# A softmax convolution, a two-dimensional Fourier mix and an MLP on one core: the low halves of the normalised rows stored as one run with shifted weight tables, the first column's fold on ScalarE, one more addition a batch on VectorE, and the mask of the weight scale taken in PSUM

## The chip, the core and the metric

The kernel runs on one core of one Trainium2 chip. The metric is the device time of one execution in microseconds (us). The engines are TensorE (PE; its weight loads are shown as PEld), VectorE (DVE), ScalarE (ACT) and GpSimd (POOL); SyncE (SP) issues every DMA. Each engine works through its own list of instructions in order and waits on semaphores for the others.

## The reference

The input is x of 8 batches, 4224 positions and 192 columns. All of it is float32 in and out.

```python
# 1. a causal convolution of 7 taps, weights by softmax, one set for each of 8 heads of 24 columns
w = softmax(weight_gen, axis=-1)                      # (8, 4224, 8, 7)
x = einsum('bshk,bskhg->bshg', w, windows_of(x, 7))   # (8, 4224, 192)
# 2. the real part of a Fourier transform over positions and columns, added
u = x + real(fft(fft(x, axis=1), axis=2))
# 3. rows normalised, then an MLP 192 -> 768 -> 192, added
un = (u - mean(u)) / sqrt(var(u) + 1e-6)
out = u + maximum(un @ w_ch1, 0) @ w_ch2
```

## The kernel before

**Tiling.** The 4224 positions of a batch are 33 rows r on 128 partitions. They are worked in nine groups g (or chunks c): eight of four rows, 128x768 elements, and a last one of a single row, 128x192. `conv(b)` (L710) makes the seven products of a chunk, `pr`, mostly on VectorE (128x768), and GpSimd adds them into `u`; with `DVE_ADDS` (L50) the first of the six additions of a chunk runs on VectorE instead, in two halves of 128x384 through PSUM tiles `ps` (`add_in_psum`, L701). Before the change that is so in chunks 2 to 7 of batch 1 alone. Then the chunk's two pairs of mirrored rows are folded into `sm`: column 0 stands apart, since columns 1 to 191 are read backwards. TensorE multiplies `sm` by a Fourier table (`pg`), the result goes through DRAM (`g_d`) and comes back as `g`; `transform(b)` (L913) and `mix(b, g)` (L961) finish the transform (`pp`, `eo`) and add it to `u`.

**Norm and MLP.** `norm(b, g)` (L987) normalises a group into `un` and splits it into two float16 parts, `hl`: the high part of the 192 columns, then the rest. Before the change the rest stands crosswise: block 1 of `hl` is high columns 128 to 191 beside low columns 128 to 191, block 2 is low columns 0 to 127. So the subtraction takes two GpSimd instructions. One transposing DMA turns `hl` into `ht`, three blocks of 128 rows for the first matrix product `ph` (tables `w1h0`, `w1l0`, `w1h1`, `w1l1` by `pieces`, L1054). ScalarE and VectorE make the hidden part `hh`, and TensorE multiplies it by the second matrix into `po`. Groups are numbered n = 9b + g. Up to n = 6 the second product is float32 with the table `w2f`; from then on it is float16 with `w2h` and `w2l`.

**Weight scales.** The matrices get a power of two as scale (`weight_scale`, L547): VectorE takes the largest word of each partition (`mx`), masks its exponent bits, takes the largest over the three pieces, TensorE carries it across partitions (`mr`), and VectorE makes the scale `sc` out of it. For the first matrix this runs at 65 to 75 us, for the second (`split_w2`, L632) at 167 to 191 us, in the middle of batch 0's MLP and batch 1's convolution.

**Order.** The code only records instructions. `plan` (L219) then places them on the engines by costs for each (`cost`, L192), dependencies, buffers and the seven PSUM banks that all products share, and `emit` (L385) writes them in that order. So a change of one instruction gives the engines another order everywhere after it. As all instructions are issued by `emit`, the profile puts them on one line, L408, and groups are told apart by tiles.

Of the kernel before, what the change touches and what calls it, by code (L numbers as in the profile page):

```python
# [11 lines left out]
F16 = mybir.dt.float16  # L12
# [37 lines left out]
DVE_ADDS = {(1, c): 1 for c in range(2, NC)}  # L50
HOLD3 = 3
WIRE = 0.5

F32_GROUPS = 7
# [405 lines left out]
def tile_dynconv_fnet_mlp(  # L460
# [52 lines left out]
    w2f = cpool.tile([P, NH, D], F32, name="w2f")  # L513
# [33 lines left out]
    def weight_scale(words, bits, nm):  # L547

        mask, unit, least, up, down = {32: (0x7F800000, 1.0, 4.0 * 2 ** 23, 257.0, -3.0),
                                       64: (0x7FF00000, 8.0, 900.0 * 2 ** 20, 1153.0, -899.0)}[bits]  # L550
        n = len(words)
        mx = cpool.tile([P, 2 * n + 2], F32, name=f"mx_{nm}")
        for i, word in enumerate(words):
            nc.vector.tensor_reduce(out=mx[:, i:i + 1], in_=word.bitcast(F32), axis=AX.X, op=ALU.max, apply_absolute_value=True)
        ex = mx[:, n:2 * n].bitcast(I32)
        nc.vector.tensor_scalar(out=ex, in0=mx[:, 0:n].bitcast(I32), scalar1=mask, scalar2=None, op0=ALU.bitwise_and)
        m1, m2 = mx[:, 2 * n:2 * n + 1], mx[:, 2 * n + 1:2 * n + 2]
        nc.vector.tensor_reduce(out=m1, in_=ex, axis=AX.X, op=ALU.max)
# [151 lines left out]
    def conv(b):  # L710
# [53 lines left out]
        for grp in groups:  # L764
# [222 lines left out]
    def norm(b, g):  # L987
# [46 lines left out]
        for t in range(T):  # L1034
# [5 lines left out]
        nc.gpsimd.tensor_tensor(out=hl[:, 0:T, 2 * P:3 * P], in0=un[:, 0:T, 0:P],  # L1040
                                in1=hl[:, 0:T, 0:P], op=ALU.subtract)
        last_lo[NG * b + g] = nc.gpsimd.tensor_tensor(out=hl[:, 0:T, D:2 * P], in0=un[:, 0:T, P:D],
                                                      in1=hl[:, 0:T, P:D], op=ALU.subtract)
# [43 lines left out]
    def first_products(n, hidden):  # L1087
# [229 lines left out]
```

## Time and profile before

| What | Before |
|---|---|
| Median of 3 runs | 1097.79 us (1095.75 to 1098.76) |
| Profiled execution | 1100.12 us, its span 1098.3 us |
| TensorE, VectorE busy | 1065.1 us, 961.5 us |
| ScalarE, GpSimd busy | 786.7 us, 871.5 us |
| TensorE's granted clock, mean | 0.991 |

The busy time of an engine is the time in which it had an instruction under way. TensorE's matmuls overlap, so a mean duration there is longer than the spacing of two matmuls. In names such as `hl<-un,hl` the tile that is written stands first.

### The profile page before, as it was taken

To read this page: it belongs to the slowest core of one execution; us is meant where nothing else is said; L and a number is where in the kernel's file an instruction comes from. 1 tells how busy PE (TensorE), PEld (TensorE's weight loads), DVE (VectorE), ACT (ScalarE), POOL (GpSimd) and SP (SyncE) were. 2 spreads that over 40 slices of the span, in tenths; PEclk is the share of its full clock that TensorE was granted. 3 is DMA by queue.
4 is the path that set the end of the run, shared out by engine and by line. 5 is a ranking of instruction groups with operands and counts; after the bars stand their busy time and mean duration, and the time that the engine had idled before them with its cause. 6 is when DMAs were issued, how large, how long until landed. Compare 5 with 4: busy or idle time off the path is not lost.

```text
span 1098.3 us, 23862 instructions
## 1 busy us (share of the span) xinstructions
PE 1065.1 (97%) x8596; PEld 807.9 (74%) x8596; DVE 961.5 (88%) x1737; ACT 786.7 (72%) x2385; POOL 871.5 (79%) x759
## 2 busy tenths in 40 slices
PE   7899997999999999999999999999999999999998
PEld 5477785788575867677777867687777777787767
DVE  7999899789999999999999999999999998345443
ACT  4666774569855797868785888778786888579841
POOL 4989799399999999699979999799969999202210
PEclk8999998999999999999999999999999999999999
DMA  8453142624475246715465266616553423622421
GB/s 300 150 161 93 50 106 89 178 63 102 113 215 135 67 130 194 155 58 138 108 204 110 71 140 182 166 53 148 111 162 95 92 65 79 135 57 70 90 57 48
DMA packets 166125, 130.20 MB, mean 119 GB/s; under 512 B 119533, under 2 KB 142710, under 8 KB 166006
## 3 DMA queue, kind: packets, MB, share of 16 engines
q1 hardware_dynamic: 166006, 128.67, 45.2%
q8 instruction: 68, 1.11, 0.4%
q14 instruction: 51, 0.42, 0.1%
HBM read 60.38 MB, written 39.43 MB: 91 GB/s over the span
## 4 chain that ended last, share of the span: by engine, by line
PE 43%; DVE 20%; POOL 19%; issue 12%; DMA 4%; ACT 2%; SPq 1%; POOLq 0%; DVEq 0%
PE po L408 18%; PE ph L408 17%; POOL u L408 15%; DVE pr L408 6%; DVE u L408 3%; DVE hh L408 3%; POOL hl L408 3%; PE eo L408 2%; PE pp L408 2%; DVE wp L408 2%; POOL sm L408 1%; PE pg L408 1%; DMA x_sb<-in_x_dram 1%; DVE mx_w L408 1%; DMA g<-g_d 1%
## 5 line engine op out<-in xcount | busy, mean ns | idle before, releaser
L408 POOL TENSOR_TENSOR u<-u,pr 128x768 f32<-128x768 f32 (+1 forms) x396 | 655.2, 1679 | 29.2 <-DVE pr L408 17.8
L408 PE MATMUL po<-w2h,hh 128*128 128x192 f16 x2832 | 416.6, 246 | 5.2 <-DVE hh L408 4.2
L408 PEld LDWEIGHTS <-hh 128*128 128x128 f16 x4248 | 364.1, 98 | 48.4 <-DVE hh L408 5.6
L408 PE MATMUL ph<-ht,w1h 128*128 128x512 f16 (+1 forms) x1296 | 391.2, 363 | 1.6 <-DMA ht<-hl 1.0
L408 DVE TENSOR_TENSOR pr<-x_sb,wp 128x768 f32<-128x768 f32 (+1 forms) x409 | 347.9, 875 | 17.6 <-POOL u L408 15.1
L408 PE MATMUL po<-w2l,hh 128*128 128x192 f16 x1416 | 347.7, 246 | 0.0
L408 ACT ACTIVATE hh<-ph 128x512 f16<-128x512 f32 (+2 forms) x400 | 221.2, 589 | 127.4 <-PE ph L408 83.8
L408 DVE SCALAR_TENSOR_TENSOR hh<-ph,hh 128x512 f16<-128x512 f32 (+1 forms) x358 | 233.0, 677 | 63.5 <-ACT hh L408 63.0
L408 PE MATMUL ph<-ht,w1l 128*128 128x512 f16 (+2 forms) x696 | 230.6, 359 | 0.0
L408 PEld LDWEIGHTS <-w1h 128*128 128x128 f16 x1296 | 127.5, 99 | 108.0 <-issue 27.4
L408 POOL TENSOR_TENSOR hl<-un,hl 128x512 f16<-128x512 f32 (+1 forms) x138 | 116.5, 859 | 70.4 <-issue 38.0
L408 ACT ACTIVATE un<-u,rs 128x192 f32<-128x192 f32 x264 | 127.0, 538 | 23.1 <-POOL rs L408 15.0
L408 ACT ACTIVATE junk<-u,st 128x192 f16<-128x192 f32 x252 | 114.2, 454 | 4.4
L408 ACT ACTIVATE junk<-u 128x192 f16<-128x192 f32 x252 | 90.8, 361 | 35.9 <-DVE u L408 32.9
L408 PEld LDWEIGHTS <-w1l 128*128 128x128 f16 (+1 forms) x864 | 64.2, 97 | 51.4 <-issue 18.5
L408 DVE SCALAR_TENSOR_TENSOR u<-po,isc,u 128x384 f32<-128x384 f32 (+1 forms) x122 | 72.8, 597 | 20.5 <-PE po L408 20.1
L408 PE MATMUL eo<-cs_sb,pq 97*128 97x97 f32 x544 | 86.2, 273 | 0.2 <-ACT pq L408 0.2
L408 PEld LDWEIGHTS eo<-cs_sb,pq 97*128 97x128 f32 x544 | 78.2, 191 | 5.8 <-issue 0.4
L408 POOL TENSOR_TENSOR sm<-u 128x382 f32<-128x382 f32 (+1 forms) x128 | 75.2, 608 | 4.2 <-ACT u L408 4.2
L408 PE MATMUL po<-w2f,hh 128*128 128x192 f32 x336 | 76.9, 333 | 0.0
L408 DVE TENSOR_TENSOR u<-u,eo 128x380 f32<-128x380 f32 (+3 forms) x160 | 71.7, 487 | 0.6
L408 PEld LDWEIGHTS po<-w2f,hh 128*128 128x128 f32 x336 | 61.8, 194 | 13.1 <-issue 0.7
(92 smaller groups left out, 1162.5 us busy)
## 6 DMA issues: line engine op xcount, KB each, us to landing
out_dram<-u SPq DMA_DIRECT2D x64, 384.0 KB
x_sb<-in_x_dram SPq DMA_DIRECT2D x48, 384.0 KB
x_sb<-in_x_dram SPq DMA_DIRECT2D x8, 864.0 KB
g<-g_d SPq DMA_DIRECT2D x40, 162.0 KB
g_d<-gt SPq DMA_DIRECT2D x32, 195.0 KB
g_d<-gt SPq DMA_DIRECT2D x32, 189.0 KB
g<-g_d SPq DMA_DIRECT2D x40, 144.0 KB
w<-in_weight_gen_dram SPq DMA_DIRECT2D x6, 924.0 KB
```

Source lines behind the costliest of these rows:

```text
L408: ins = getattr(getattr(nc, op.engine), op.call)(*map(found, op.args), **{n: found(a) for n, a in op.kw.items()}).ins
```

## The change

There are four edits. (1) **Halves one behind the other:** from n = 9 on, one GpSimd subtraction writes the low part of all 192 columns behind the high part. The rows of `ht` are thereby another set, so two copies of the high table with shifted rows are made (`w1s`, four DMAs from `w1h0` and `w1h1`, in the place of `w2f`, which no later group reads). (2) **Column 0's fold** is done by ScalarE in two instructions of 128x1 with the mirrored value as bias, in all eight batches; GpSimd did it in one of 128x2. (3) **One addition a batch:** chunk 3 of batches 2 to 7 has its first addition on VectorE through PSUM. (4) **The scale's mask:** the maximum over the three pieces is taken first, on unmasked words; the mask and what follows it work on two columns of the PSUM bank that holds `mr`.

```diff
+DVE_ADDS = {**{(1, c): 1 for c in range(2, NC)}, **{(b, 3): 1 for b in range(2, 8)}}
+ACT_FOLDS = range(8)
+LINEAR = 9
...
     def weight_scale(words, bits, nm):
-        ex = mx[:, n:2 * n].bitcast(I32)
-        nc.vector.tensor_scalar(out=ex, in0=mx[:, 0:n].bitcast(I32), scalar1=mask, scalar2=None, op0=ALU.bitwise_and)
-        m1, m2 = mx[:, 2 * n:2 * n + 1], mx[:, 2 * n + 1:2 * n + 2]
-        nc.vector.tensor_reduce(out=m1, in_=ex, axis=AX.X, op=ALU.max)
+        m1 = mx[:, n:n + 1]
+        nc.vector.tensor_reduce(out=m1, in_=mx[:, 0:n], axis=AX.X, op=ALU.max)
         row = pst("ph", [P, P], F32, f"mr_{nm}")
         nc.tensor.matmul(row, lhsT=m1.broadcast_to([P, P]), rhs=ident32, start=True, stop=True)
-        nc.vector.tensor_reduce(out=m2, in_=row, axis=AX.X, op=ALU.max)
-        nc.vector.tensor_scalar_max(out=m2, in0=m2, scalar1=least)
+        top, word = row[:, 0:1], row[:, 1:2].bitcast(I32)
+        nc.vector.tensor_reduce(out=top, in_=row, axis=AX.X, op=ALU.max)
+        nc.vector.tensor_scalar(out=word, in0=top.bitcast(I32), scalar1=mask, scalar2=None, op0=ALU.bitwise_and)
+        nc.vector.tensor_scalar_max(out=top, in0=word, scalar1=least)
...
     def conv(b):
-                    last_fold[b] = nc.gpsimd.tensor_tensor(out=sm[:, :, 0], in0=u[:, 0:2, 0], in1=u[:, 3:1:-1, 0],
-                                                           op=ALU.add)
+                    if b in ACT_FOLDS:
+                        for j in range(2):
+                            nc.scalar.activation(sm[:, j, 0:1], u[:, j, 0:1], AF.Identity, bias=u[:, 3 - j, 0:1])
...
     def norm(b, g):
+        if NG * b + g >= LINEAR:
+            last_lo[NG * b + g] = nc.gpsimd.tensor_tensor(out=hl[:, 0:T, D:2 * D], in0=un[:, 0:T], in1=hl[:, 0:T, 0:D], op=ALU.subtract)
+        else:
...
+    def linear_tables():
+        w1s = cpool.tile([P, 2, DFF], F16, name="w1s", tag="w2f")
+        for dst, src in ((w1s[0:64, 0], w1h1[0:64]), (w1s[64:P, 0], w1h0[0:64]),
+                         (w1s[0:64, 1], w1h0[64:P]), (w1s[64:P, 1], w1h1[64:P])):
+            nc.sync.dma_start(dst, src)
+        tables[:] = w1s[:, 1], w1s[:, 0]
+    def pieces():
+        return ((w1h0, 0), (w1l0, 0), (tables[0], 2), (tables[1], 1), (w1l1, 1))
...
     def mlp(n):
+        if n == LINEAR:
+            linear_tables()
```

The order that the plan makes of it is shown at three places. The first is VectorE at the second matrix's scale (`mx_w`, `mr_w`), beside chunk 7 of batch 1's convolution (`pr_7`); before:

```order
L408 TENSOR_REDUCE mx_w_391_1749<-w2f_937 128x1
L408 TENSOR_TENSOR pr_7_4_428_1860<-x_sb_71,wp_166_643 128x768
L408 TENSOR_SCALAR mx_w_391_1749<-mx_w_391_1749 128x3
L408 TENSOR_REDUCE mx_w_391_1749<-mx_w_391_1749 128x1
L408 TENSOR_TENSOR gt_4_362_1768<-pg_5_384_1853,up_8_69 128x2x97
L408 TENSOR_TENSOR gt_4_362_1768<-pg_5_384_1853,up_8_69 128x2x95
L408 RECIPROCAL rs_7_398_1868<-rs_7_398_1868 128x4
L408 TENSOR_TENSOR pr_7_5_430_1883<-x_sb_71,wp_166_643 128x768
```

and now:

```order
L410 TENSOR_TENSOR pr_7_3_427_1851<-x_sb_71,wp_166_645 128x768
L410 TENSOR_REDUCE mx_w_391_1747<-mx_w_391_1747 128x1
L410 TENSOR_TENSOR pr_7_4_428_1863<-x_sb_71,wp_166_645 128x768
L410 TENSOR_TENSOR pr_7_5_430_1879<-x_sb_71,wp_166_645 128x768
L410 TENSOR_TENSOR gt_4_362_1767<-pg_5_384_1869,up_8_69 128x2x97
L410 TENSOR_TENSOR gt_4_362_1767<-pg_5_384_1869,up_8_69 128x2x95
L410 TENSOR_TENSOR pr_7_6_437_1898<-x_sb_71,wp_166_645 128x768
L410 SCALAR_TENSOR_TENSOR u_3_77_452<-po_3_2_375_1818,sc_w_185_747,u_3_77_452 128x384
L410 TENSOR_REDUCE mr_w_392_1906<-mr_w_392_1906 128x1
L410 TENSOR_TENSOR wp_166_645<-w_167_145,wp_166_645 128x56
L410 TENSOR_SCALAR mr_w_392_1906<-mr_w_392_1906 128x1
```

The masking step on 128x3 is gone from its place ahead of the maximum, a step of 128x1 on the bank `mr_w` stands further down, and the maximum moved up by one product.

The second is GpSimd in batch 2's convolution, chunks 2 to 4, beside the norm of batch 1 (`hl_1`, `hl_2`); before:

```order
L408 TENSOR_TENSOR sm_2_549_2680<-u_2_529_2351 128x2x191
L408 TENSOR_TENSOR sm_2_549_2680<-u_2_529_2351 128x2
L408 TENSOR_TENSOR u_3_553_2466<-u_3_553_2466,pr_3_3_564_2558 128x768
L408 TENSOR_TENSOR u_4_584_2682<-u_4_584_2682,pr_4_1_585_2692 128x768
L408 TENSOR_TENSOR hl_1_544_2717<-un_1_534_2686,hl_1_544_2717 128x4x128
L408 TENSOR_TENSOR hl_1_544_2717<-un_1_534_2686,hl_1_544_2717 128x4x64
L408 TENSOR_TENSOR rs_2_557_2735<-st_2_556_2631,rs_2_557_2735 128x4
L408 TENSOR_TENSOR u_3_553_2466<-u_3_553_2466,pr_3_4_565_2581 128x768
L408 TENSOR_TENSOR u_4_584_2682<-u_4_584_2682,pr_4_2_586_2726 128x768
L408 TENSOR_TENSOR u_3_553_2466<-u_3_553_2466,pr_3_5_568_2628 128x768
```

and now:

```order
L410 TENSOR_TENSOR sm_2_549_2606<-u_2_529_2343 128x2x191
L410 TENSOR_TENSOR u_3_553_2472<-u_3_553_2472,pr_3_6_580_2679 128x768
L410 TENSOR_TENSOR u_4_586_2708<-u_4_586_2708,pr_4_1_587_2725 128x768
L410 TENSOR_TENSOR hl_1_544_2752<-un_1_534_2699,hl_1_544_2752 128x4x192
L410 TENSOR_TENSOR rs_2_559_2766<-st_2_558_2667,rs_2_559_2766 128x4
L410 TENSOR_TENSOR u_4_586_2708<-u_4_586_2708,pr_4_2_588_2738 128x768
L410 TENSOR_TENSOR sm_3_583_2770<-u_3_553_2472 128x2x191
L410 TENSOR_TENSOR u_4_586_2708<-u_4_586_2708,pr_4_3_597_2780 128x768
L410 TENSOR_TENSOR u_4_586_2708<-u_4_586_2708,pr_4_4_599_2793 128x768
L410 TENSOR_TENSOR hl_2_577_2851<-un_2_561_2804,hl_2_577_2851 128x4x192
```

The fold of 128x2 has left the list, the subtraction is one row of 128x4x192, and chunk 3 (`u_3`) is added up ahead of chunk 4 where the two took turns.

The third is SyncE, where the output of group 6 (`u_6`) and the first transposition of batch 1 (`ht_0`) are issued; before:

```order
L408 DMA x_sb_71<-in_x_dram 128x384
L408 DMA out_dram<-u_6_110_452 128x768
L408 DMA g_d_0_18_165<-gt_0_497_2423 65x768
L408 DMA g_d_0_18_165<-gt_0_497_2423 63x768
L408 DMA_TRANSPOSE ht_0_520_2589<-hl_0_519_2515 128x12x128
L408 DMA hd_0_521_2658<-ht_0_520_2589 64x4x128
```

and now:

```order
L410 DMA x_sb_71<-in_x_dram 128x384
L410 DMA w1s_2527<-w1h_12_819 64x768
L410 DMA w1s_2527<-w1h_10_834 64x768
L410 DMA w1s_2527<-w1h_12_819 64x768
L410 DMA w1s_2527<-w1h_10_834 64x768
L410 DMA out_dram<-u_6_110_461 128x768
L410 DMA g_d_0_18_165<-gt_0_497_2422 65x768
L410 DMA g_d_0_18_165<-gt_0_497_2422 63x768
L410 DMA_TRANSPOSE ht_0_520_2659<-hl_0_519_2537 128x12x128
L410 DMA out_dram<-u_7_133_698 128x768
L410 DMA hd_0_521_2727<-ht_0_520_2659 64x4x128
```

Four copies into `w1s` now stand ahead of the output, the two stores to `g_d` and the transposition.

## Rows read from the trace of the kernel before

**Rows 1.** The page, part 1: busy time of each engine, share, instructions.

```profile
PE 1065.1 (97%) x8596; PEld 807.9 (74%) x8596; DVE 961.5 (88%) x1737; ACT 786.7 (72%) x2385; POOL 871.5 (79%) x759
```

**Rows 2.** Windows of 120 us: length, busy us of each engine (instructions), clock, DMA.

```profile
240.00:360.00 120.00, 115.18 (x946) 85.71 (x945) 114.96 (x202) 90.19 (x268) 115.47 (x99) 0.99 0.52 130
...
480.00:600.00 120.00, 118.67 (x1029) 89.41 (x1027) 116.28 (x204) 94.47 (x280) 111.79 (x97) 1.00 0.53 133
```

**Rows 3.** Timeline around 180 us by engine: start us, us, engine, instruction [idle before].

```profile
177.44 8.83 POOL L408 TENSOR_TENSOR u<-u,pr 128x768 f32<-128x768 f32 x5
...
178.36 8.89 DVE L408 TENSOR_SCALAR mx_w<-mx_w 128x3 int32<-128x3 int32 x1
...
179.71 0.38 PE L408 MATMUL ph<-ht,w1l 128*128 128x512 f16 x1
187.50 0.79 PE L408 MATMUL mr_w<-ident,mx_w 128*128 128x128 f32 x2 [7.42 <-DVE mx_w L408]
...
190.28 0.62 ACT L408 ACTIVATE w2h<-w2f,sc_w 128x384 f16<-128x384 f32 x1 [10.84 <-DVE sc_w L408]
```

**Rows 4.** The tile mx_w: engine, duration ns min/median/max of its mask and maximum steps.

```profile
L408 DVE TENSOR_SCALAR mx_w<-mx_w x4: 149/156/8894, 68.1 to 189.9; 128x3 int32<-128x3 int32 x2, 128x1 f32<-128x1 f32 x2
```

**Rows 5.** Windows on TensorE alone: length, busy us (instructions), clock, DMA share, GB/s.

```profile
187.60:193.40 5.80, 5.80 (x17) 0.50 0.73 212
193.60:199.40 5.80, 5.80 (x33) 1.00 0.68 266
```

**Rows 6.** Waits of POOL from 187 to 203 us; timelines of SP and PE after it.

```profile
POOL u L408 <- DVE pr L408: 6.3, 4, 2.2
...
202.08 0.33 SPq L408 DMA_DIRECT2D x_sb<-in_x_dram  x1
202.58 3.23 SPq L408 DMA_TRANSPOSE ht<-hl  x1
...
209.93 0.38 PE L408 MATMUL ph<-ht,w1h 128*128 128x512 f16 x1 [0.97 <-DMA ht<-hl]
```

**Rows 7.** Groups by shape, whole span: count | busy us, mean ns | idle before.

```profile
L408 POOL TENSOR_TENSOR u<-u,pr 128x768 f32<-128x768 f32 x348 | 627.7, 1827 | 24.1 <-DVE pr L408 13.7 <-PE po L408 5.7 <-DVE rs L408 2.9
...
L408 DVE TENSOR_TENSOR pr<-x_sb,wp 128x768 f32<-128x768 f32 x361 | 332.0, 946 | 9.1 <-POOL u L408 6.8 <-PE pa L408 1.4 <-DMA x_sb<-in_x_dram 0.6
...
L408 POOL TENSOR_TENSOR hl<-un,hl 128x512 f16<-128x512 f32 x61 | 71.1, 1166 | 63.9 <-issue 36.9 <-ACT hl L408 25.2 <-DMA g_d<-gt 1.7
...
L408 POOL TENSOR_TENSOR hl<-un,hl 128x256 f16<-128x256 f32 x61 | 41.4, 679 | 0.0
...
L408 POOL TENSOR_TENSOR sm<-u 128x2 f32<-128x2 f32 x64 | 13.4, 209 | 0.0
...
L408 DVE TENSOR_TENSOR u<-ps,u 128x384 f32<-128x384 f32 x12 | 6.2, 547 | 0.0
L408 DVE TENSOR_TENSOR ps<-x_sb,wp 128x384 f32<-128x384 f32 x12 | 6.2, 553 | 0.0
...
L408 ACT ACTIVATE rs<-st,eps_t 128x1 f32<-128x1 f32 x8 | 2.3, 294 | 0.1
```

**Rows 8.** Chain that ended last, its share by line from 213 to 320 us.

```profile
by line: POOL u L408 44.0%; issue 28.5%; POOL hl L408 5.7%; DVE pr L408 5.3%; DVE hh L408 4.4%; POOL sm L408 4.2%; DVE u L408 2.9%; DVE wp L408 2.3%; PE po L408 1.1%; PE ph L408 0.8%; DVE eo L408 0.5%; ACT un L408 0.5%; POOL rs L408 0.5%; D
```

**Rows 9.** The same stretch: additions, folds and subtractions on POOL.

```profile
L408 POOL TENSOR_TENSOR u<-u,pr 128x768 f32<-128x768 f32 x47 | 84.2, 1822 | 3.5 <-DVE pr L408 3.3
...
L408 POOL TENSOR_TENSOR hl<-un,hl 128x512 f16<-128x512 f32 x5 | 5.8, 1169 | 0.0
...
L408 POOL TENSOR_TENSOR sm<-u 128x2 f32<-128x2 f32 x7 | 1.4, 200 | 0.0
```

**Rows 10.** Waits of TensorE from 200 to 360 us, and from 360 us on.

```profile
PE po L408 <- DVE hh L408: 4.2, 6, 1.8
...
PE pp L408 <- DMA g<-g_d: 3.4, 3, 1.2
```

**Rows 11.** Waits of ScalarE for GpSimd, whole span: us in total, times, longest.

```profile
ACT un L408 <- POOL rs L408: 15.0, 18, 2.1
```

More of the change, by code (lines that the diff above doesn't have):

```diff
@@ L49 @@
 POOL_TAPS = {(0, 0): (5, 6), (0, 1): (5, 6), (0, 3): (6,), (1, 0): range(7), (1, 1): range(7)}
-DVE_ADDS = {(1, c): 1 for c in range(2, NC)}
+DVE_ADDS = {**{(1, c): 1 for c in range(2, NC)}, **{(b, 3): 1 for b in range(2, 8)}}
 HOLD3 = 3
+ACT_FOLDS = range(8)
+LINEAR = 9
 WIRE = 0.5
@@ L512, in tile_dynconv_fnet_mlp @@
     w2l = cpool.tile([P, NH, D], F16, name="w2l")
-    w2f = cpool.tile([P, NH, D], F32, name="w2f")
+    w2f = cpool.tile([P, NH, D], F32, name="w2f", tag="w2f")
     isc = cpool.tile([P, 1], F32, name="isc")
@@ L551, in weight_scale @@
         n = len(words)
-        mx = cpool.tile([P, 2 * n + 2], F32, name=f"mx_{nm}")
+        mx = cpool.tile([P, n + 1], F32, name=f"mx_{nm}")
         for i, word in enumerate(words):
             nc.vector.tensor_reduce(out=mx[:, i:i + 1], in_=word.bitcast(F32), axis=AX.X, op=ALU.max, apply_absolute_value=True)
-        ex = mx[:, n:2 * n].bitcast(I32)
-        nc.vector.tensor_scalar(out=ex, in0=mx[:, 0:n].bitcast(I32), scalar1=mask, scalar2=None, op0=ALU.bitwise_and)
-        m1, m2 = mx[:, 2 * n:2 * n + 1], mx[:, 2 * n + 1:2 * n + 2]
-        nc.vector.tensor_reduce(out=m1, in_=ex, axis=AX.X, op=ALU.max)
+        m1 = mx[:, n:n + 1]
+        nc.vector.tensor_reduce(out=m1, in_=mx[:, 0:n], axis=AX.X, op=ALU.max)
         row = pst("ph", [P, P], F32, f"mr_{nm}")
         nc.tensor.matmul(row, lhsT=m1.broadcast_to([P, P]), rhs=ident32, start=True, stop=True)
-        nc.vector.tensor_reduce(out=m2, in_=row, axis=AX.X, op=ALU.max)
-        nc.vector.tensor_scalar_max(out=m2, in0=m2, scalar1=least)
+        top, word = row[:, 0:1], row[:, 1:2].bitcast(I32)
+        nc.vector.tensor_reduce(out=top, in_=row, axis=AX.X, op=ALU.max)
+        nc.vector.tensor_scalar(out=word, in0=top.bitcast(I32), scalar1=mask, scalar2=None, op0=ALU.bitwise_and)
+        nc.vector.tensor_scalar_max(out=top, in0=word, scalar1=least)
         sc = cpool.tile([P, 2], I32, name=f"sc_{nm}")
-        nc.vector.tensor_scalar(out=sc[:, 0:1], in0=m2, scalar1=-unit, scalar2=up * 2 ** 23,
+        nc.vector.tensor_scalar(out=sc[:, 0:1], in0=top, scalar1=-unit, scalar2=up * 2 ** 23,
                                 op0=ALU.mult, op1=ALU.add)
-        nc.vector.tensor_scalar(out=sc[:, 1:2], in0=m2, scalar1=unit, scalar2=down * 2 ** 23,
+        nc.vector.tensor_scalar(out=sc[:, 1:2], in0=top, scalar1=unit, scalar2=down * 2 ** 23,
                                 op0=ALU.mult, op1=ALU.add)
@@ L882, in conv @@
                     sm = sb.tile([P, 2, D], F32, tag="fold", name=f"sm_{b}_{c}", bufs=3)
-                    nc.gpsimd.tensor_tensor(out=sm[:, :, 1:D], in0=u[:, 0:2, 1:D], in1=u[:, 3:1:-1, D - 1:0:-1],
+                    last_fold[b] = nc.gpsimd.tensor_tensor(out=sm[:, :, 1:D], in0=u[:, 0:2, 1:D], in1=u[:, 3:1:-1, D - 1:0:-1],
                                             op=ALU.add)
-                    last_fold[b] = nc.gpsimd.tensor_tensor(out=sm[:, :, 0], in0=u[:, 0:2, 0], in1=u[:, 3:1:-1, 0],
-                                                           op=ALU.add)
+                    if b in ACT_FOLDS:
+                        for j in range(2):
+                            nc.scalar.activation(sm[:, j, 0:1], u[:, j, 0:1], AF.Identity, bias=u[:, 3 - j, 0:1])
+                    else:
+                        last_fold[b] = nc.gpsimd.tensor_tensor(out=sm[:, :, 0], in0=u[:, 0:2, 0], in1=u[:, 3:1:-1, 0],
+                                                               op=ALU.add)
                 t2 = 2 * c + 1 if R > 1 else 0
@@ L1039, in norm @@
         nc.scalar.copy(hl[:, 0:T, 0:D], un[:, 0:T, :])
[L1040 to L1043, printed above, removed]
+        if NG * b + g >= LINEAR:
+            last_lo[NG * b + g] = nc.gpsimd.tensor_tensor(out=hl[:, 0:T, D:2 * D], in0=un[:, 0:T], in1=hl[:, 0:T, 0:D], op=ALU.subtract)
+        else:
+            nc.gpsimd.tensor_tensor(out=hl[:, 0:T, 2 * P:3 * P], in0=un[:, 0:T, 0:P],
+                                    in1=hl[:, 0:T, 0:P], op=ALU.subtract)
+            last_lo[NG * b + g] = nc.gpsimd.tensor_tensor(out=hl[:, 0:T, D:2 * P], in0=un[:, 0:T, P:D],
+                                                          in1=hl[:, 0:T, P:D], op=ALU.subtract)
         ht = sb.tile([P, 4, 3, P], F16, tag="ht", name=f"ht_{b}_{g}", bufs=3)
@@ L1052, in norm @@
         yield 2.0
-    pieces = ((w1h0, 0), (w1l0, 0), (w1h0, 2), (w1h1, 1), (w1l1, 1))
+    tables = [w1h0, w1h1]
+    def linear_tables():
[6 more added lines that the diff above has]
+        return ((w1h0, 0), (w1l0, 0), (tables[0], 2), (tables[1], 1), (w1l1, 1))
     def full_products(ph, c, ht, T, which, start, stop):
@@ L1102, in first_products @@
                         hidden.extend(relu_split(n, phs[k], 1, T, k))
-                for i, mm in enumerate(full_products(phs[c], c, ht, T, pieces[:-1], c < NH // 2, c >= NH // 2)):
+                for i, mm in enumerate(full_products(phs[c], c, ht, T, pieces()[:-1], c < NH // 2, c >= NH // 2)):
                     if i == 0 and n - (c == 0) in last_ph:
@@ L1116, in first_products @@
                 at = c % span * T
-                for i, mm in enumerate(full_products(ph[:, at:at + T], c, ht, T, pieces, True, True)):
+                for i, mm in enumerate(full_products(ph[:, at:at + T], c, ht, T, pieces(), True, True)):
                     if i == 0 and n > PAIRED:
```

## The prediction

> **What bounds the kernel now.** I read the page's busy times first, then windows of 120 us, then the waits of TensorE, and the timeline only where TensorE stands still. TensorE is busy 97% of the span [rows 1]. In a window of steady work it is busy 118.67 of 120 us, VectorE 116.28, GpSimd 111.79 and ScalarE 94.47; between 240 and 360 us TensorE has 115.18 [rows 2]. The change takes nothing off TensorE's own work, so it can win only time in which TensorE waits or runs slowly. From 360 us on its largest wait is 3.4 us in all, three waits for `g` from DRAM; between 200 and 360 us it is 4.2 us for `hh` of VectorE [rows 10]. The one large hole lies at 180 us, and there one VectorE instruction stands behind everything.
>
> **The hole at 180 us.** The mask of the second weight scale, 128x3, runs 8.89 us from 178.36 [rows 3]; the median of the four such steps is 0.156 us [rows 4]. GpSimd starts five additions in a row at 177.44 and is at them for 8.83 us [rows 3]. The mask ends with GpSimd's run, not with its own work: I read it as a wait for SBUF access that GpSimd holds. TensorE's last matmul ahead of it starts at 179.71, then TensorE waits 7.42 us for the scale's carry `mr_w`, and ScalarE waits 10.84 us for the scale [rows 3]. After it TensorE's granted clock is 0.50, its 1.2 GHz level, for 5.80 us: 17 matmuls, where the next 5.80 us at 1.00 (2.4 GHz) hold 33 [rows 5]. What the half clock cost is 5.80 x (1 - 17/33) = 2.8 us. The hole is 7.4 + 2.8 = 10.2 us of TensorE.
>
> The Trainium skill says on this, in "SBUF — State Buffer", section "Who interferes with whom", that a tensor_scalar between SBUF operands may use the port pair that VectorE shares with GpSimd, that whoever starts first has it for that whole instruction and the other blocks until it ends, and that an instruction with PSUM operands stays off it. By "for that whole instruction" the mask should wait for the rest of one addition only, some 0.9 us, and the edit would win about that. The row has the wait last over all five additions, so I follow the row for the length, and the page only for the escape through PSUM, which no run shows yet.
>
> **Edit 4, the mask in PSUM.** The step of 128x3 in SBUF goes; the new one of 128x1 has no row with both ends in PSUM. Its bounds are 0.15 us, the least of the masking and maximum steps, and 8.89 us, the same wait again [rows 4]. I take 0.15, since three of the four small steps took that. So 8.7 us leave VectorE and 10.2 us of hole leave TensorE. What is late next? GpSimd worked through the hole, so its work after it comes earlier only by what it then idled: 6.3 us in four waits for products between 187 and 203 us [rows 6]. Two folds of column 0 in that stretch fall away, 0.2 us each: 6.7 us. The transposition that TensorE needs at 209.93 is issued at 202.58, right behind a load of x at 202.08 [rows 6]; that load overwrites rows which the convolution's last products read, and these need buffers that GpSimd's additions free. So I let this transposition come 6.7 us earlier, not 10.2. TensorE, 10.2 us early, then waits 3.5 us longer there than the 0.97 us of before, and the gain is 6.7 us. Bounds: 2.2 us, if only the longest of the four waits [rows 6] goes, and 10.2 + 0.97 = 11.2 us, if `ht` keeps up.
>
> **Edits 1 to 3 on GpSimd.** An addition of 128x768 is 1827 ns, the fold of column 0 209 ns [rows 7]. The subtraction takes 1166 ns for 128x512 and 679 ns for 128x256 [rows 7]; the slope is 487/256 = 1.90 ns an element, so one of 128x768 is about 1166 + 256 x 1.90 = 1653 ns (an estimate from these rows), 0.19 us less than the two. Over the run: 6 x 1.83 = 11.0, 64 x 0.209 = 13.4, and 63 x 0.19 = 12.0 us; 36 of GpSimd's 871.5 us. It counts only where GpSimd is on the path. That is 213 to 320 us: additions are 44.0% of the chain there and "issue" between GpSimd's instructions much of the rest [rows 8]. In that stretch lie batch 2's chunk 3, seven folds and five subtractions of four-row groups [rows 9]: 1.82 + 7 x 0.20 + 5 x 0.19 = 4.2 us. TensorE can take of it no more than it waits for `hh`, 4.2 us [rows 10], and VectorE, which makes `hh`, gets more work. I take half of 4.2, 2 us; bounds 0 and 4.2. From 360 us on TensorE has no room but the 3.4 us for `g`, which an earlier end of the folds may shorten; I take 1 us of it, bounds 0 and 3.4.
>
> **What is added.** VectorE: an addition through PSUM replaces one product of 946 ns by two of 553 and two additions of 547 [rows 7], 1.25 us a batch and 7.5 us in six. Its cover is the idle 3.7 us in a window of 120 [rows 2]; without it the price is 7.5 us. I take 0, as the cover is three times the need. The two `ps` tiles also take two of seven PSUM banks for about 1.1 us a batch (twice 0.55); no row prices that, so the end is the same 7.5 us. ScalarE: 128 instructions; the nearest is the 128x1 activation with a column as bias, 294 ns [rows 7], so at most 128 x 0.294 = 38 us, 16 x 0.294 = 4.7 us a batch, covered by 25.5 us of idle time a window [rows 2]. I take 0; what it costs if the fold waits for GpSimd is a rival below. In the first 120 us, where the eight folds of batch 0 move, I take 0 within 2 us either way: 8 x 0.2 less on GpSimd against 4.7 us more on ScalarE. SyncE: four copies into `w1s` stand ahead of two stores and batch 1's first transposition. At 0.33 us an issue [rows 6] they are 1.3 us; TensorE may be waiting there, or the queue idle. I take half, 0.6 us, bounds 0 and 1.3. The first product with `w1s` comes behind that transposition, so their landing is covered by its own.
>
> **The sum.** -6.7 - 2 - 1 + 0.6 = -9.1 us. Against the profiled execution, 1100.12 us with 1.8 us around its span, that is 1091.0 us. This execution lies 2.3 us above the median of the three runs, 1097.79; against the median the forecast is 1088.7 us.
>
> **Rivals.**
> *Everything keeps up.* The transposition moves with TensorE, and the waits for `hh` and `g` go: 10.2 + 0.97 + 4.2 + 3.4 = 18.8 us, 1079.0. For it: GpSimd loses 36 us of work. Against it: those waits end on VectorE and on DRAM, which get no faster.
> *The hole closes and opens elsewhere.* Only 2.2 us of GpSimd's idling goes, and VectorE's 7.5 us reach TensorE in part; or the wait lasted because of what the page says not, and the mask in PSUM meets it too. The time is between 1095.6 and 1097.8. For it: GpSimd is full from 213 us on, and a backlog does not shrink because VectorE is early. Against it: three like steps took 0.15 us.
> *Slower: ScalarE stands behind GpSimd.* ScalarE's list is in order, and relu for `hh` and the copies out of `pq` and `pg` stand behind each fold. Today it waits for GpSimd's `rs` in 18 of 61 groups, 15.0 us in all [rows 11], 15.0/61 = 0.25 us a group. If each of the 56 folds of batches 1 to 7 waits 0.25 us and all of it reaches TensorE, it costs 14 us: 1088.7 + 14 = 1102.7. It decides from (9.1 + 3.3)/56 = 0.22 us a fold. For it: one late addition holds up three other engines. Against it: ScalarE idles 25.5 us of 120, and the largest waits of TensorE end on VectorE and DRAM, not on ScalarE [rows 10].
>
> **How the numbers follow.** Forecast 0.58, all keeps up 0.15, elsewhere 0.17, slower 0.10. The range of 1079 to 1097 leaves out a third of the second case, a third of the third and the fourth: 0.05 + 0.05 + 0.10. A measurement of this kernel tells about 0.3%, 3.3 us, from no change. Faster is the forecast, the second case and half of the third, 0.58 + 0.15 + 0.08 = 0.81; the other 0.09 is the same; slower 0.10.
>
> **What would show it.** In the profile after: the masking step near 0.15 us, no wait of TensorE for `mr_w` and no window at 0.50 after 180 us; the wait for `ht` some 6 to 8 us earlier than 209.93 and longer than 0.97 us; a fold on GpSimd of 128x382 alone and subtractions near 1.65 us; batches 2 to 7 in windows as full on TensorE as now. I am wrong if the masking step is long again, if TensorE loses at the next transposition all that it won, or if its waits for `hh` from 360 us on come to several us, with ScalarE's waits for `u` ahead of them.

## The result and the profile after

The changed kernel takes 1084.25 us (median of five runs), the kernel before 1097.4 us in the same session, 13.2 us more. The forecast was 1088.7 us. One run of the changed kernel at 1103.79 us, with a mean granted clock of 0.947, is left out of the ratio, which is 0.9875 with an interval of 0.9859 to 0.9892, or 11.9 to 15.5 us less; the median of the other four runs is 1083.3 us. The profiled execution after took 1081.15 us, that of before 1100.12 us. They differ by 18.9 us: the profile of before lies 2.7 us above its median, the one of after 3.1 us below. Whatever is read from the two traces has to be set against 18.9 us.

The page after, busy times and, from part 4, the chain that ended last, which answer to [rows 1]:

```profile
PE 1058.2 (98%) x8596; PEld 806.3 (75%) x8596; DVE 953.7 (88%) x1755; ACT 810.6 (75%) x2513; POOL 844.0 (78%) x626
...
PE 71%; DVE 18%; ACT 3%; POOL 3%; DMA 2%; issue 2%; SPq 0%; DVEq 0%; POOLq 0%; ACTq 0%
```

GpSimd's 871.5 us have become 844.0, ScalarE's 786.7 have become 810.6, and seven tenths of the chain are TensorE's own work. The windows after, as in [rows 2], and one over the stretch of the hole; the columns are length, then busy time and instructions of TensorE, its weight loads, VectorE, ScalarE and GpSimd, the granted clock, and DMA:

```profile
180.00:195.00 15.00, 14.93 (x84) 11.74 (x83) 11.83 (x30) 9.82 (x25) 14.84 (x16) 1.00 0.78 247
...
240.00:360.00 120.00, 117.46 (x991) 87.03 (x990) 117.63 (x211) 95.00 (x304) 111.03 (x82) 1.00 0.52 137
480.00:600.00 120.00, 119.60 (x1052) 91.44 (x1050) 118.30 (x210) 96.20 (x298) 108.81 (x79) 1.00 0.50 132
```

The same 15 us from 180 on before the change:

```profile
180.00:195.00 15.00, 7.58 (x27) 5.65 (x27) 14.96 (x24) 4.01 (x8) 11.70 (x10) 0.66 0.44 138
```

TensorE is busy 14.93 us there instead of 7.58, at full clock instead of 0.66. The timeline after around 180 us answers to [rows 3], and the last line, from the tile's own view, to [rows 4]:

```profile
174.16 10.70 POOL L410 TENSOR_TENSOR u<-u,pr 128x768 f32<-128x768 f32 x6
...
179.84 0.38 PE L410 MATMUL mr_w<-ident,mx_w 128*128 128x128 f32 x2
...
181.29 0.17 DVE L410 TENSOR_SCALAR mr_w<-mr_w 128x1 int32<-128x1 int32 x1
...
182.86 0.24 DVE L410 TENSOR_TENSOR isc<-sc_w,sc_w 128x1 f32<-128x1 f32 x1
...
182.47 0.61 ACT L410 ACTIVATE w2h<-w2f,sc_w 128x384 f16<-128x384 f32 x1 [0.31 <-DVE sc_w L410]
...
L410 DVE TENSOR_SCALAR mr_w<-mr_w x4: 156/158/166, 72.5 to 182.1; 128x1 int32<-128x1 int32 x2, 128x1 f32<-128x1 int32 x2
```

GpSimd is in a long row of additions as before, and the mask in PSUM takes 0.17 us beside them. TensorE does not wait for `mr_w` (7.42 us before), and ScalarE waits 0.31 us for the scale instead of 10.84. The line on `isc` is the one that the prediction did not look at; the experiments lead to it.

Waits of TensorE after, from 200 to 360 us (the first two lines) and from 360 us on (the third), and ScalarE's wait for GpSimd, which answer to [rows 10, 11]:

```profile
PE pp L410 <- DMA g<-g_d: 3.0, 3, 1.3
PE ph L410 <- DVE u L410: 0.9, 2, 0.7
...
PE pp L410 <- DMA g<-g_d: 0.4, 1, 0.4
...
L410 ACT ACTIVATE un<-u,rs 128x192 f32<-128x192 f32 x264 | 130.2, 540 | 19.2 <-POOL rs L410 11.3
```

To see where the time went I cut both runs at the starts of four of VectorE's 136 `u<-po` steps, which add the MLP's result: numbers 4, 8, 32 and 132, counted from 0. A group of four rows has two of them, a single row one, so the cuts are the first steps of groups 2 and 4 and the second steps of groups 16 and 69 (groups counted from 0). The table has all the experiments too. "Mask" and "isc" are the durations in that run's trace of the two VectorE steps around 180 us that make the second weight scale: the mask, and the product of two columns `isc<-sc_w,sc_w`.

| kernel | mask, us | isc, us | groups 2 to 4 | 4 to 16 | 16 to 69 |
|---|---|---|---|---|---|
| before | 8.89 | 1.81 | 42.2 | 186.9 | 701.5 |
| after | 0.17 | 0.24 | 31.1 | 187.1 | 692.6 |
| edit 4 alone | 0.16 | 6.42 | 36.1 | 185.1 | 700.9 |
| after without edit 4 | 0.72 | 0.34 | 31.1 | 187.2 | 693.2 |
| after without edit 2 | 0.17 | 0.35 | 31.6 | 185.3 | 699.8 |
| after without edit 1 | 0.16 | 9.74 | 40.4 | 186.9 | 698.5 |
| after without edit 3 | 0.16 | 9.63 | 40.2 | 188.8 | 694.4 |
| before, mask on one column | 0.15 | 6.31 | 35.9 | 186.7 | 701.5 |
| before, other order of TensorE | 7.05 | 0.65 | 40.1 | 188.3 | 699.6 |
| edit 2 alone | 7.16 | 1.55 | 39.7 | 185.0 | 701.7 |
| edit 3 alone | 8.91 | 1.81 | 40.9 | 186.7 | 696.9 |
| edits 2 and 3 | 0.16 | 0.33 | 31.2 | 185.8 | 700.2 |

Of the 18.9 us, 42.2 - 31.1 = 11.1 are the hole at 180 us. Between groups 4 and 16 nothing is won or given back (186.9 and 187.1). The steady work behind gives 701.5 - 692.6 = 8.9 us. The rest, 0.9 us the other way, lies nearly all ahead of group 2. The table is one trace a kernel, and the run of before in it is at the upper end of its kernel's times, so a difference from before can be some 3 us larger there than between the medians.

### The profile page after: what moved, and what is told of

Read it like the earlier page. It is cut to its first block, busy times and chain, and to the rows that moved or that the text cites. A ratio compares the mean times of both kernels' runs of the same rounds, so it can differ in the third digit from the quotient of the medians.

```text
span 1079.4 us, 23828 instructions
## 1 busy us (share of the span) xinstructions
PE 1058.2 (98%) x8596; PEld 806.3 (75%) x8596; DVE 953.7 (88%) x1755; ACT 810.6 (75%) x2513; POOL 844.0 (78%) x626
## 4 chain that ended last, share of the span: by engine, by line
PE 71%; DVE 18%; ACT 3%; POOL 3%; DMA 2%; issue 2%; SPq 0%; DVEq 0%; POOLq 0%; ACTq 0%
PE po L410 29%; PE ph L410 29%; DVE pr L410 6%; PE pp L410 4%; PE eo L410 4%; DVE u L410 3%; POOL u L410 3%; PE pg L410 3%; DVE wp L410 2%; DVE hh L410 2%; PE pa L410 1%; DMA g<-g_d 1%; ACT pr L410 1%; DVE gt L410 1%; DVE pa_w L410 1%
## 5 line engine op out<-in xcount | busy, mean ns | idle before, releaser
L410 POOL TENSOR_TENSOR u<-u,pr 128x768 f32<-128x768 f32 (+1 forms) x390 | 644.5, 1669 | 25.2 <-DVE pr L410 14.0
L410 PE MATMUL po<-w2h,hh 128*128 128x192 f16 x2832 | 421.5, 246 | 0.2
L410 DVE TENSOR_TENSOR pr<-x_sb,wp 128x768 f32<-128x768 f32 (+1 forms) x403 | 339.8, 872 | 10.1 <-POOL u L410 6.9
L410 PE MATMUL ph<-ht,w1s 128*128 128x512 f16 (+1 forms) x756 | 231.6, 361 | 0.0
L410 PE MATMUL ph<-ht,w1h 128*128 128x512 f16 (+1 forms) x540 | 186.4, 362 | 0.3 <-DVE bn L410 0.3
L410 POOL TENSOR_TENSOR hl<-un,hl 128x768 f16<-128x768 f32 (+3 forms) x75 | 105.8, 1413 | 74.9 <-ACT hl L410 39.7
L410 ACT ACTIVATE un<-u,rs 128x192 f32<-128x192 f32 x264 | 130.2, 540 | 19.2 <-POOL rs L410 11.3
L410 PEld LDWEIGHTS <-w1s 128*128 128x128 f16 x756 | 74.4, 99 | 55.3
L410 PEld LDWEIGHTS <-w1h 128*128 128x128 f16 x540 | 52.8, 98 | 51.0 <-issue 25.1
L410 ACT COPY pq<-pp 97x204 f32<-97x204 f32 (+3 forms) x176 | 47.0, 315 | 34.7 <-PE pp L410 30.6
```

The costliest lines, as they stand in the source:

```text
L410: ins = getattr(getattr(nc, op.engine), op.call)(*map(found, op.args), **{n: found(a) for n, a in op.kw.items()}).ins
```

## The experiments

**One edit, and all but one.** Five kernels, against a median of before of 1096.7 us, for the one without edit 3 of 1097.03 us.

Edit 4 alone, in before:

```diff
-        nc.vector.tensor_scalar(out=ex, in0=mx[:, 0:n].bitcast(I32), scalar1=mask, ...)
+        top, word = row[:, 0:1], row[:, 1:2].bitcast(I32)
+        nc.vector.tensor_scalar(out=word, in0=top.bitcast(I32), scalar1=mask, ...)
```

> The kernel before with edit 4 alone; the order of the engines is the one of before but for the moved mask. Theory A (the mask waited for GpSimd's hold on SBUF and with PSUM operands it does not): the masking step takes about 0.15 us, TensorE has no wait for mr_w near 180 us and no window at half clock after it, and of the 10.2 us about 8 to 9 reach the end: 1088 to 1090 us. Rival B (the hole is closed but the next transposition of ht gives most of it back): 1093 to 1096 us. Rival C (the wait had another cause): 1097 us and a long masking step again.

Measured: 1094.39 us, ratio 0.9977 (0.9964 to 0.9989), 2.3 us of the 6.7 that the prediction gave it. (The profiled pair, 1100.12 and 1093.67 us, is 6.4 us apart.) Timeline of this kernel:

```profile
179.38 8.97 POOL L408 TENSOR_TENSOR u<-u,pr 128x768 f32<-128x768 f32 x5
188.26 1.04 POOL L408 TENSOR_TENSOR sm<-u 128x382 f32<-128x382 f32 x1
189.21 1.85 POOL L408 TENSOR_TENSOR u<-u,pr 128x768 f32<-128x768 f32 x1
190.97 0.25 POOL L408 TENSOR_TENSOR sm<-u 128x2 f32<-128x2 f32 x1
...
184.65 6.42 DVE L408 TENSOR_TENSOR isc<-sc_w,sc_w 128x1 f32<-128x1 f32 x1
...
192.38 0.59 PE L408 MATMUL po<-w2f,hh 128*128 128x192 f32 x2 [3.01 <-DVE w2l L408]
```

The first hole is closed, and a second one has opened ahead of 192 us. The product `isc`, one element a partition from two columns in SBUF, takes 6.42 us and ends at 191.07, where GpSimd's row of long instructions gives way to a fold of 0.25 us. VectorE's `w2l` stands behind `isc` in its list, and TensorE waits 3.01 us for that.

The other four take one edit back out of the changed kernel:

```diff
-        top, word = row[:, 0:1], row[:, 1:2].bitcast(I32)       # e2: weight_scale of before
-ACT_FOLDS = range(8)                       # e3
+ACT_FOLDS = ()
-LINEAR = 9                                 # e4
+LINEAR = 10 ** 6
-DVE_ADDS = {..., **{(b, 3): 1 for b in range(2, 8)}}    # e5
+DVE_ADDS = {(1, c): 1 for c in range(2, NC)}
```

> The changed kernel with edit 4 undone. Theory A: the masking step of 128x3 waits for a run of GpSimd additions again, 4 to 9 us, and the time goes up by 7 to 10 us to 1091 to 1094 us. If edits 1 to 3 had made room for the wait, the time stays within 3 us of 1084.

> The changed kernel with column 0's fold on GpSimd in all batches. If the fold's 0.2 us on GpSimd counts in steady work: 1 to 4 us slower than the changed kernel, 1085 to 1088 us. Rival: the two instructions on ScalarE hold back other work and their removal makes it 1 to 4 us faster, 1080 to 1083 us. Rival: TensorE is full either way, no difference beyond 2 us.

> The changed kernel with two subtractions a group and no w1s tables. If GpSimd's 0.19 us a group counts: 1 to 4 us slower, 1085 to 1088 us. Rival: TensorE is full either way and the four copies into w1s are gone too: within 2 us of 1084.

> The changed kernel with the first addition of chunk 3 back on GpSimd in batches 2 to 7. If GpSimd is what keeps TensorE waiting at each batch's transform, 2 to 5 us slower than the changed kernel, 1086 to 1089 us. Rival: VectorE's 7.5 us cost more than GpSimd's 11 us gain, then 1 to 4 us faster. Rival: no difference beyond 2 us.

Measured: without edit 4 1082.77 us (0.9883, 0.9858 to 0.9907), without edit 2 1087.32 (0.9917, 0.9903 to 0.9932), without edit 1 1083.81 (0.9882, 0.9868 to 0.9896), without edit 3 1087.65 (0.9907, 0.9878 to 0.9936). So edit 4, on which the forecast rested, is not missed when the other three are there: 0.9883 against 0.9875, with intervals that overlap. The runs of three of these kernels fall in two groups: without edit 3, 1082.19, 1082.24 and 1084.26 us, then 1091.04, 1091.11 and 1091.54; without edit 4, five from 1080.96 to 1084.32 and one of 1091.15; without edit 1, four from 1083.39 to 1084.42 and one of 1094.71. The profiles of the slower kind are at hand for two, without edit 1 (1094.71) and without edit 3 (1091.11). Timelines of the one and, in the second block, of the other:

```profile
187.55 1.04 POOL L410 TENSOR_TENSOR sm<-u 128x382 f32<-128x382 f32 x1
188.50 1.85 POOL L410 TENSOR_TENSOR u<-u,pr 128x768 f32<-128x768 f32 x1
190.26 1.83 POOL L410 TENSOR_TENSOR hl<-un,hl 128x512 f16<-128x512 f32 x2
192.00 1.04 POOL L410 TENSOR_TENSOR sm<-u 128x382 f32<-128x382 f32 x1
193.40 0.59 POOL L410 TENSOR_TENSOR u<-u,pr 128x192 f32<-128x192 f32 x1 [0.36 <-DVE pr L410]
...
183.31 9.74 DVE L410 TENSOR_TENSOR isc<-sc_w,sc_w 128x1 f32<-128x1 f32 x1
...
193.84 1.01 PE L410 MATMUL po<-w2f,hh 128*128 128x192 f32 x2 [5.62 <-DVE w2l L410]
```

```profile
190.48 0.98 POOL L410 TENSOR_TENSOR sm<-u 128x382 f32<-128x382 f32 x1
191.43 0.19 POOL L410 TENSOR_TENSOR rs<-st,rs 128x4 f32<-128x4 f32 x1
...
181.86 9.63 DVE L410 TENSOR_TENSOR isc<-sc_w,sc_w 128x1 f32<-128x1 f32 x1
...
192.28 1.01 PE L410 MATMUL po<-w2f,hh 128*128 128x192 f32 x2 [5.08 <-DVE w2l L410]
```

In both `isc` is stuck until GpSimd stands idle or starts a short instruction, and TensorE waits 5.1 to 5.6 us. In the traces of the faster kind (after, without edit 4, without edit 2) `isc` takes 0.24 to 0.35 us. So one kernel has two times, and in the traces they go with whether this one step gets in: 1091.11 - 1082.24 = 8.9 us without edit 3, 11.0 without edit 1, 8.5 without edit 4, by the medians of the two groups. That the unprofiled runs of the slower kind have the same cause is inferred from their times. Taken by the faster group alone, the medians without edit 4, 1 and 3 are 1082.7, 1083.7 and 1082.2 us, within 1.1 us of the changed kernel's 1083.3; only without edit 2 is every run at 1085.8 us or above.

**Order alone, and the mask on one column in SBUF.** Both start from before:

```diff
-VISIT = 98                                 # e8: TensorE's list in another order
+VISIT = 90
-        nc.vector.tensor_reduce(out=m1, in_=ex, ...)           # e6: maximum first, then the mask on 128x1
+        nc.vector.tensor_reduce(out=m1, in_=mx[:, 0:n], ...)
+        nc.vector.tensor_scalar(out=ex, in0=m1.bitcast(I32), scalar1=mask, ...)
+        nc.vector.tensor_scalar_max(out=m1, in0=ex, scalar1=0.0)
```

> The kernel before with its instructions unchanged and another order: the planner's constant for a visit of the half products is 90 instead of 98, which moves about a fifth of TensorE's list. It measures what another order alone is worth. If order alone is worth little, within 2 us of 1097. If the gain of the changed kernel beyond the hole is of the order and not of the work taken off GpSimd, this moves by 3 to 6 us either way.

> The kernel before with the mask taken after the maximum, on 128x1 instead of 128x3, and still in SBUF; a further step of 128x1 makes a number of it. The order is that of before. If a step of one element a partition never takes the shared access, it needs 0.15 us and the hole at 180 us is gone as in the run with the mask in PSUM; if SBUF at both ends is enough to make it wait, it is 5 to 9 us again.

Another order: 1097.45 us, ratio 1.0004 (0.9993 to 1.0015). This new order by itself is worth nothing; the mask was stuck again. The mask on one column: one run of 1092.95 us. Its lines, the first of the new order, the others of the one column:

```profile
175.88 7.05 DVE L408 TENSOR_SCALAR mx_w<-mx_w 128x3 int32<-128x3 int32 x1
```

```profile
177.86 0.15 DVE L408 TENSOR_SCALAR mx_w<-mx_w 128x1 int32<-128x1 int32 x1
...
182.08 6.31 DVE L408 TENSOR_TENSOR isc<-sc_w,sc_w 128x1 f32<-128x1 f32 x1
...
189.17 0.59 PE L408 MATMUL ph<-ht,w1h 128*128 128x512 f16 x1 [3.16 <-DVE w2l L408]
```

On one column the mask runs freely in SBUF, so it is the three columns that wait and PSUM is not needed. And again `isc` takes the mask's place.

**Edits 2 and 3 without the rest.** By then I held that the whole gain came from work taken off GpSimd. Edit 2 moves 64 folds ([rows 7]), not 27 as the text on it below has it.

```diff
+DVE_ADDS = {**{(1, c): 1 for c in range(2, NC)}, **{(b, 3): 1 for b in range(2, 8)}}   # e10, e11
+ACT_FOLDS = range(8)                                                                   # e9, e11
```

> The kernel before with edits 2 and 3 alone: the first columns' folds on ScalarE and one addition a batch on VectorE; the mask stays in SBUF and the halves are subtracted in two pieces. Theory GpSimd: the whole gain comes from what these two take off GpSimd, so the median is 1083 to 1086 us (11 to 14 below before), and TensorE waits under 1 us for g from 360 us on. Rival, the prediction's own sizes: these two are worth about 2 to 3 us together, so 1093 to 1095 us. The two are 8 us apart.

> The kernel before with edit 2 alone: 27 folds of the first columns (128x2, about 0.2 us each on GpSimd) become pairs of ScalarE steps. Theory GpSimd with effects that add up: about half of the gain, 1090 to 1092 us. Theory GpSimd with a threshold (either edit is enough to bring GpSimd below TensorE's pace, as each costs only 3 us when it is left out of the changed kernel): 1086 to 1088 us. Rival, the prediction's sizes: 1095 to 1096 us.

> The kernel before with edit 3 alone: one addition a batch (1.8 us) of six batches on VectorE. Theory GpSimd with effects that add up: about half of the gain, 1090 to 1092 us. Theory GpSimd with a threshold: 1086 to 1088 us. Rival, the prediction's sizes: 1095 to 1096 us.

Measured against 1097.51 us: both 1093.66 (0.9955, 0.9936 to 0.9974), edit 2 alone 1096.11 (0.9985, 0.9975 to 0.9996), edit 3 alone 1094.15 (0.9968, 0.9953 to 0.9982). That theory fell: the two are worth 3.9 us, near the 3 that the prediction gave to edits 1 to 3. The profiled run with both, 1087.88 us, was the fastest of ten, which go up to 1096.95, and its trace shows what was different from edit 2 or edit 3 alone:

```profile
171.91 0.16 DVE L409 TENSOR_SCALAR mx_w<-mx_w 128x3 int32<-128x3 int32 x1
...
183.28 0.33 DVE L409 TENSOR_TENSOR isc<-sc_w,sc_w 128x1 f32<-128x1 f32 x1
```

Here both steps got in, without edit 4, and groups 2 to 4 took 31.2 us. With edit 2 or edit 3 alone the mask was stuck for 7.16 and 8.91 us.

**Two probes.** A tail behind the changed kernel's last output, when the other engines have no work left, starts a small VectorE step beside GpSimd additions. The cut is from the first probe.

```diff
+            nc.gpsimd.tensor_tensor(out=tok, in0=got, in1=got, op=ALU.add)
+            for ...: nc.gpsimd.tensor_tensor(out=acc, in0=acc, in1=add_on, op=ALU.add)
+            nc.vector.tensor_scalar(out=got.bitcast(I32)[:, 0:3], in0=tok.bitcast(I32)[:, 0:3], scalar1=mask, ...)
```

> The changed kernel with a tail: GpSimd runs 1, 2, 5, 5, 5, 5, 5 and 10 additions of 128x768 without a pause, and as each run begins VectorE gets one small step. In order: mask 128x3 in SBUF against 1, 2 and 5 additions, mask 128x1 against 5, mask 128x3 with its output in PSUM against 5, a product of two SBUF columns 128x1 against 5, mask 128x4 against 5, mask 128x3 against 10. If access is given back only when GpSimd's run ends, the masks in SBUF of 128x3 and 128x4 take about 1.8, 3.6, 9, 9 and 18 us; if it is given back after each addition, each takes at most 1.8 us. The steps of 128x1 and into PSUM should take 0.15 to 0.2 us, and the product of two columns up to 1.8 us.

The planner moved most of the additions ahead, so that only one stood beside each of the first seven steps, and ten beside the last. Timeline of VectorE: the third step, 128x3 beside one addition, then 128x1, 128x3 into PSUM, the product of two columns, and 128x3 beside ten additions.

```profile
1100.48 1.75 DVE L410 TENSOR_SCALAR got<-tok 128x3 int32<-128x3 int32 x1 [0.31 <-POOL tok L410]
1102.54 0.15 DVE L410 TENSOR_SCALAR got<-tok 128x1 int32<-128x1 int32 x1 [0.31 <-POOL tok L410]
1104.45 0.17 DVE L410 TENSOR_SCALAR q_bank<-tok 128x3 int32<-128x3 int32 x1 [1.76 <-POOL tok L410]
...
1106.37 1.74 DVE L410 TENSOR_TENSOR got<-tok 128x1 f32<-128x1 f32 x1 [1.56 <-POOL tok L410]
...
1110.48 1.75 DVE L410 TENSOR_SCALAR got<-tok 128x3 int32<-128x3 int32 x1 [0.31 <-POOL tok L410]
```

Three columns in SBUF and a product of two SBUF columns wait for an addition; one column, or a result in PSUM, does not. `isc` is of the kind that waits. But none waited longer than one addition. The second probe kept the chains together and asked whether additions on two accumulators, as in before, leave no gap:

> The changed kernel with a tail that measures the mask by itself, after its last output: six times a 128x3 mask of VectorE in SBUF that becomes free to start just as a chain of GpSimd additions (128x768, about 1.8 us each) starts: five on one accumulator, five that alternate between two accumulators, one, two on two accumulators, ten that alternate, ten on one. Theory 1, the hole of the kernel before was long because additions on two accumulators leave no gap in which VectorE gets in: the mask takes about 1.8 us beside chains on one accumulator, and about 9 and 18 us beside the five and the ten that alternate. Theory 2, access is handed back after one addition whatever it writes: 1.8 us in all six, and the hole of 8.9 us before had another cause, which stays open.

Timelines: GpSimd's additions five and ten times on one accumulator, and VectorE's masks beside five on one accumulator, five that alternate, and ten on one.

```profile
1096.23 9.32 POOL L410 TENSOR_TENSOR qa<-qa,qx 128x768 f32<-128x768 f32 x5
1138.08 18.73 POOL L410 TENSOR_TENSOR qa<-qa,qx 128x768 f32<-128x768 f32 x10
...
1096.31 1.75 DVE L410 TENSOR_SCALAR got<-tok 128x3 int32<-128x3 int32 x1 [0.33 <-POOL tok L410]
1105.74 1.75 DVE L410 TENSOR_SCALAR got<-tok 128x3 int32<-128x3 int32 x1 [7.68 <-POOL tok L410]
...
1138.17 1.75 DVE L410 TENSOR_SCALAR got<-tok 128x3 int32<-128x3 int32 x1 [15.99 <-POOL tok L410]
```

All six took 1.75 us, whatever the chain. That idea fell as well.

## Why the prediction was right, and where not

**The hole, right.** It was sized at 10.2 us of TensorE, with 2.8 us of half clock in it. Groups 2 to 4 are 11.1 us shorter in after, and the two groups of runs of one kernel, which go with a stuck `isc`, are 8.5 to 11.0 us apart. One reading was off: the mask does not end with the five additions, at 186.27, but at 187.25, with the fold behind them:

```profile
186.24 0.98 POOL L408 TENSOR_TENSOR sm<-u 128x382 f32<-128x382 f32 x1
```

**The give-back, wrong.** The step that took 10.2 down to 6.7 was that the transposition which TensorE needs next "come 6.7 us earlier, not 10.2". It was issued at 191.68 instead of 202.58, 10.9 us earlier, TensorE had no wait for `ht` there, and from group 4 to 16 all twelve traces lie between 185.0 and 188.8 us. A hole closed at 180 us stays closed; the upper bound of 11.2 was the end to take. The line of SyncE's queue after:

```profile
190.32 0.33 SPq L410 DMA_DIRECT2D x_sb<-in_x_dram  x1
191.68 2.34 SPq L410 DMA_TRANSPOSE ht<-hl  x1
```

**What is late next, wrong.** This is the step that failed. For "What is late next?" I went to GpSimd's backlog and the load on SyncE. The next late thing was further on in the same chain on VectorE, just behind the scales: `isc`, a product that reads two SBUF operands beside the same GpSimd run. Its row in before was there to be read:

```profile
191.43 1.81 DVE L408 TENSOR_TENSOR isc<-sc_w,sc_w 128x1 f32<-128x1 f32 x1
```

1.81 us for one element is a wait for one addition: GpSimd's runs beside it from 191.41 for 1.81 us. With the mask out of the way `isc` comes some 7 us earlier, into the middle of GpSimd's run. Edit 4 alone therefore bought 2.3 us, and the rival "the hole closes and opens elsewhere" is what happened to it: 1094.39 us, just below that rival's 1095.6 to 1097.8, though by a step that the rival does not name. The Trainium skill, "SBUF — State Buffer", section "Who interferes with whom", which the prediction drew on for the mask alone, names a VectorE instruction with two SBUF inputs as one that contends with GpSimd. The product of the first probe and `isc` agree with that (1.74 us beside one addition). The rule of the Trainium skill that the prediction set aside, in the same section, that the lock is held for one instruction, agrees with the twelve waits of the probes, none over 1.75 us, and not with the eight waits of 6.31 to 9.74 us in the table.

**So the total was nearly right for another reason.** The forecast had the hole closed by edit 4. Its sum has 6.7 us for a hole that is 11.1 in the traces, 2 where nothing was won and 1 for what became 8.9; that its 9.1 us come near the measured 13.2 is in part luck. What the runs show is a hole that is closed when both steps get in. With edits 1, 2 and 3 GpSimd's and VectorE's instructions stand otherwise against each other, and `isc`, and without edit 4 the mask too, usually gets in. It need not meet a gap for that: in after `isc` starts some 0.24 us ahead of the end of one of six additions in a row, and is done with that addition, while the row goes on to 184.86. Without edit 1 it starts just as far ahead of the end of an addition (at 183.31, the addition ends at 183.55) and takes 9.74 us. So why it gets in is not shown. No sum over edits gives these times: without edit 4 there is no clear loss, edit 4 alone gains 2.3 us, edits 2 and 3 alone 3.9, and each set of three loses at most 4.6 (0.9917 against 0.9875, without edit 2). Edit 1 alone was not run.

**Edits 1 to 3 on GpSimd.** The prediction's 2 us for 213 to 320 us are not there: the stage from group 4 to 16 is unchanged (186.9 and 187.1), although TensorE's waits for `hh` from 200 to 360 us, 4.2 us before, are down to 0.3. Its waits for `g` in that stretch rose from 0.3 to 3.0 us. The first line is before, the second after:

```profile
PE pp L408 <- DMA g<-g_d: 0.3, 1, 0.3
...
PE eo L410 <- DVE hh L410: 0.3, 1, 0.3
```

The 1 us from 360 us on was too small: groups 16 to 69 take 8.9 us less, of which the waits for `g`, 3.4 to 0.4 us, name 3.0. Which wait the remaining 6 us were, TensorE's own waits do not name. The table has a pattern, from one profile each: the three kernels with both edits 1 and 2 need 692.6 to 694.4 us there, the nine others 696.9 to 701.7. For edit 2 the run times bear it out, since without it no run is under 1085.8 us. For edit 1 they do not: its profile is of the one slower run, and the other four runs without it take 1083.4 to 1084.4 us, as the changed kernel does. What edit 2 needs beside it is open; with edit 3 and both steps in, the stage still takes 700.2 us.

**What is added, right.** The fold on ScalarE takes 288 ns and one addition through PSUM 552 + 543 ns a half, as costed. The first line below is the fold, the second the subtraction:

```profile
L410 ACT ACTIVATE sm<-u 128x1 f32<-128x1 f32 x128 | 33.4, 288 | 3.5 <-POOL u L410 3.4
...
L410 POOL TENSOR_TENSOR hl<-un,hl 128x768 f16<-128x768 f32 x56 | 92.3, 1648 | 68.2 <-ACT hl L410 34.1 <-issue 34.1
```

The subtraction of 128x768 came at 1648 ns against the estimate of 1653. The four copies into `w1s` took SyncE 2.42 us from 238.66 us on, against the 1.3 of the prediction, but TensorE had no wait for `ht` or `w1s` from 236 to 258 us, so the 0.6 us added for them are not there. The rival "ScalarE stands behind GpSimd" put 0.25 us on each fold: the 128 steps waited 3.4 us for `u` in all, and ScalarE's waits for `rs` fell from 15.0 to 11.3 us. "Everything keeps up" gave 18.8 us less; the profiled pair differs by 18.9, the medians by 13.2. The transposition did keep up, but the nearness of 18.8 and 18.9 is luck: the stage with its 4.2 us for `hh` got no shorter, and it had 3.4 us for what became 8.9.

## What to carry to other kernels

When one instruction is stuck on a shared resource, list the next instructions on that engine that need the same resource before you book the whole hole: a duration far above the work (1.81 us for one element) marks them in the trace. If a gain hangs on one step getting in, look at the single run times, for two groups of them 9 us apart say more than an edit-by-edit sum. And leave-one-out and one-alone runs disagree in such a case, so both are needed before a gain is put down to an edit.

## What the runs showed of the hardware

VectorE's steps that meet GpSimd's additions wait in two ways. Beside the probes' additions they all took 1.74 to 1.75 us, one addition, whether the row had one or ten. In four kernels `isc` took 0.24 to 0.35 us and ended with the addition under way, while the next one followed without a pause. In the kernels eight steps waited 6.31 to 9.74 us, over four to nine GpSimd instructions. All eight ended within 0.03 us of the end of a long GpSimd instruction behind which GpSimd was idle or had one of 0.25 us or less (a fold of 128x2, or `rs`). The two `isc` waits with short folds still on GpSimd lasted 6.31 and 6.42 us, the two with the folds on ScalarE 9.63 and 9.74, so edit 2 may lengthen the wait where it occurs; no run was made for that. What decides whether access comes back after one instruction or only with the end of the run stays open. In the probes the number of accumulators did not, and the place within the addition at which the step begins does not seem to: 0.24 us ahead of an addition's end, with more instructions right behind it, `isc` took 0.24 us in after and 9.74 us without edit 1. The probes ran with the other engines idle, and whether that is the difference was not tried.

TensorE's granted clock takes part in the price. Before, the 15 us from 180 us on had 0.66 on average, after it 1.00, and the mean over a run, 0.992 in the median of the runs of before, was 0.995 to 0.997 in the four runs of after that the ratio uses.
